# Fifty-six products behind the last one of a spectral mixing and MoE kernel

## The chip, the cores and the metric

The kernel runs on one core of a Trainium2 chip. The metric is the device time of one execution in microseconds (us), from the program's first instruction to its last; the time of a kernel is the median of several runs. Engines are named as the profile names them: PE is TensorE's products and PEld its weight loads, DVE is VectorE, ACT is ScalarE, POOL is GpSimd, SP is SyncE; SPq and ACTq are the queues from which transfers (DMAs) are issued.

## The reference

The input `x` is 8 x 3136 x 256. It goes through a real Fourier transform along 3136, a complex 256 x 256 mixing with bias, a soft threshold and the inverse transform. A second part mixes along the sequence at rank 32 and along the channels by a two-layer network, with a residual.

```python
X = np.fft.rfft(x, axis=1)
Yr = Xr @ w_r - Xi @ w_i + b_r
Yi = Xr @ w_i + Xi @ w_r + b_i
Yr = np.sign(Yr) * np.maximum(np.abs(Yr) - lam, 0.0)     # the same for Yi
y = np.fft.irfft(Y, n=x.shape[1], axis=1)
h = y.transpose(0, 2, 1) @ U @ V
u = y + h.transpose(0, 2, 1)
out = u + np.maximum(u @ w_ch1, 0.0) @ w_ch2
```

## The kernel before, in words

The transform of 3136 = 49 x 64 points is done as products with constant matrices in four steps (a, b, c, d in the names `psa`, `psb`, `psc`, `psd`, with the mixing in `psq` and `pst` between b and c). The channel network works on 49 windows of 512 tokens: its first layer writes `psx`, `psy` and `psz`, its second layer the two banks `pso` (`l2_chunks`, lines 1567 to 1595). Most products are in fp32r and in three parts, high by high, low by high and high by low, so that nearly fp32 accuracy comes out; some are in plain fp32, and the profile shows two instructions for each of those.

The Python code first records all operations in a `_Program` (line 165). Its `order` (line 255) plans them with costs and due times, and `trace` (line 506) then gives them out in the order of their planned starts; so nearly all instructions of the profile carry line 517. After `prog.order()` in line 1714 the pools are opened, and line 1721 gives the program out. The pool `ps_f` has three PSUM banks with the tags `psf.0` to `psf.2`; the pools `ps_m` and `ps_o` hold the other banks.

The end of the program is this. The second layer of the last window in turn, window 47, ends with a chunk whose six products are sorted so that the bank `pso_0` is complete before `pso_1` (line 1582). `o_unit` (line 1598) adds each bank to the window `xq` on VectorE, `out_unit` (line 1606) transposes each half into the tile `os`, and four transfers take `os` to the output, two from the queue of SyncE and two from the queue of ScalarE (line 1616). After that the program closes with a barrier over the five engines. The last use of the banks `psf.*` is the rank-32 product `psv` of that window, some 30 us ahead of the end. The first-layer weights lie in `w1t`, 128 partitions with 7 x 2 x 512 numbers each.

Of the kernel before, what the change touches and what calls it, by code (L numbers as in the profile page):

```python
# [13 lines left out]
F32 = mybir.dt.float32  # L14
# [150 lines left out]
class _Program:  # L165
# [339 lines left out]
    def trace(self, engines, junk):  # L505
        def real(v):
            return v.get() if isinstance(v, _View) else v

        for op in sorted(self.ops, key=lambda o: (o.start, o.n)):
            if op.fill:  # L510
                o = op.out.buf.get()
                while len(o.shape) > 2:
                    o = o[:, 0]
                for _ in range(op.fill):
                    engines["pe"].matmul(o[:, 0:128], lhsT=junk, rhs=junk, start=True, stop=True)
            call = getattr(engines[op.eng], op.name)
            call(*[real(a) for a in op.args], **{k: real(a) for k, a in op.kw.items()})  # L517


@with_exitstack  # L520
def fft_mix_moe_kernel(
# [19 lines left out]
    nc = tc.nc  # L541
    prog = _Program()
    act, dve, pool, pe, dma = [prog.engine(e) for e in ("act", "dve", "pool", "pe", "sp")]
    const, dram = _Pool("const", 1), _Pool("dram", 1, "dram")
    ps_f, ps_m, ps_o = _Pool("ps_f", 3, "psum"), _Pool("ps_m", 1, "psum"), _Pool("ps_o", 1, "psum")
# [42 lines left out]
    w1t = const.tile([128, 7, 2, 512], F32R, name="w1t", tag="w1")  # L588
# [1078 lines left out]
    for w, prev, next_w in zip(turn_w, [None] + turn_w, turn_w[1:] + [None]):  # L1667
        b, j = divmod(w, NW)
        if j == 0 and b < NB:
            assert not side  # L1670
            side = [(6.5, lambda b=b: rest_unit(b))]
            if b + 1 < NB:
                start, mid, end = (1, 58, 84) if b else (18, 71, 86)
# [13 lines left out]
        for g in range(2):  # L1687
            l1s = l1_chunks(w, g)
            new = l2_chunks(w, g)
            for k in range(4):  # L1690
                for c in range(2):
                    n = WS * j + 8 * g + 2 * k + c
# [26 lines left out]
    make_identity(nc, ident.get())  # L1719
    with tc.manual_schedule():  # L1720
        prog.trace(engines, ident.get())


def _dft_constants():
# [81 lines left out]
```

## Time and profile before

| | us |
|---|---|
| median of three runs | 1691.04 |
| lowest and highest of them | 1690.72, 1691.92 |
| the profiled execution, from first to last instruction (its span) | 1691.6 |
| PE busy in it | 1678.4 (99%) |
| DVE busy in it | 1320.9 (78%) |
| mean granted TensorE clock | 0.996 of full speed |

The page lists nothing of the profiled execution outside its span, so the span stands for its own time; it is 0.56 us above the median. In the views, a row of the timeline gives the start, the duration, the engine, the line, the operation, what is written and read (`pso<-rl,w2t` is written into `pso` from `rl` and `w2t`), the shapes and a count. Products overlap: each of 512 columns shows a duration of about 0.40 us, while its neighbour starts 0.23 us later. So the rate of a series is read from its starts, and the duration of one product tells when the last of a series is finished.

### The profile page before, as it was taken

What the parts mean: (1) busy time and instruction counts of PE and PEld (TensorE: products, weight loads), DVE (VectorE), ACT (ScalarE), POOL (GpSimd) and SP (SyncE); (2) the same over time, 40 slices, a digit from 0 to 9 for tenths busy, and PEclk for the clock granted to TensorE, in tenths of its full rate; (3) what the DMA queues carried; (4) which work ended last, traced back from release to release, by engine and by line L of the source; (5) the groups of instructions that cost most, each with busy time, mean ns of one, the idle gap of its engine ahead of it and who ended that gap; (6) DMA issues with size and microseconds to landing.
All of it is one profiled execution on the core that took longest, in us unless ns stands there. A gap on an engine that the chain in (4) does not pass through costs nothing.

```text
span 1691.6 us, 31458 instructions
## 1 busy us (share of the span) xinstructions
PE 1678.4 (99%) x11104; PEld 1513.1 (89%) x11104; DVE 1320.9 (78%) x2487; ACT 1015.6 (60%) x2187; POOL 574.7 (34%) x502
## 2 busy tenths in 40 slices
PE   9999999999999999999999999999999999999998
PEld 6979998999898998999988989999989999998887
DVE  7788898589856989679875788868985689866775
ACT  4765765556666665556666666555666566554443
POOL 2312553133534443123443444223343233312221
PEclk9989999999999999999999999999999999999999
DMA  9763444324553444413464344422455234420221
GB/s 260 240 220 90 136 128 125 96 73 116 157 170 111 127 141 117 121 51 89 118 193 132 118 141 121 137 59 74 120 155 167 76 92 110 114 69 10 77 57 38
DMA packets 243449, 200.64 MB, mean 119 GB/s; under 512 B 131387, under 2 KB 192609, under 8 KB 243293
## 3 DMA queue, kind: packets, MB, share of 16 engines
q1 hardware_dynamic: 240654, 197.77, 40.9%
q8 instruction: 89, 1.46, 0.4%
q10 hardware_dynamic: 2638, 0.86, 0.2%
q14 instruction: 68, 0.55, 0.1%
HBM read 121.36 MB, written 77.20 MB: 117 GB/s over the span
## 4 chain that ended last, share of the span: by engine, by line
PE 97%; DMA 1%; DVE 1%; issue 0%; SPq 0%; ACT 0%; DVEq 0%
PE pso L517 32%; PE psy L517 18%; PE psx L517 8%; PE psq L517 7%; PE psd L517 7%; PE psa L517 6%; PE psb L517 5%; PE psc L517 4%; PE psz L517 4%; PE pst L517 4%; PE psv L517 1%; DMA xx<-in_x_dram 0%; DMA fb<-in_fb_dram 0%; PE psu L517 0%; DMA out_dram<-os 0%; DVE t0t L517 0%
## 5 line engine op out<-in xcount | busy, mean ns | idle before, releaser
L517 PE MATMUL pso<-rh,w2t 128*128 128x512 f32 x1568 | 433.6, 398 | 0.0
L517 PEld LDWEIGHTS pso<-rh,w2t 128*128 128x128 f32 x1568 | 275.6, 188 | 44.5
L517 PE MATMUL pso<-rl,w2t 128*128 128x512 f32 x784 | 246.9, 396 | 0.3 <-DVE rl L517 0.3
L517 DVE SCALAR_TENSOR_TENSOR ys<-tb,rl 64x256 f32<-64x256 f32 x350 | 197.4, 564 | 12.2 <-ACT rl L517 6.8
L517 POOL TENSOR_TENSOR yl<-ys,yh 128x512 fp32r<-128x512 f32 (+1 forms) x101 | 137.3, 1359 | 189.6 <-ACT yh L517 172.1
L517 POOL TENSOR_TENSOR xl<-xt,xh 98x512 fp32r<-98x512 f32 x96 | 130.1, 1355 | 207.0 <-ACT xh L517 195.9
L517 PEld LDWEIGHTS pso<-rl,w2t 128*128 128x128 f32 x784 | 147.6, 188 | 35.7 <-DVE rl L517 0.7
L517 DVE SCALAR_TENSOR_TENSOR rl<-s,rh 128x512 fp32r<-128x512 f32 x196 | 155.8, 801 | 5.1 <-ACT rh L517 2.9
L517 ACT ACTIVATE rh<-s 128x512 fp32r<-128x512 f32 x196 | 121.7, 629 | 57.8 <-DVE s L517 56.6
L517 POOL TENSOR_TENSOR tl<-ts,th 128x256 fp32r<-128x256 f32 x88 | 71.2, 810 | 203.9 <-ACT th L517 140.3
L517 PE MATMUL psq<-wmt,xsh 128*128 128x256 f32 (+1 forms) x704 | 130.3, 282 | 0.0
L517 PE MATMUL psy<-odh,w1t 128*128 128x256 f32 x784 | 126.3, 283 | 0.0
L517 DVE TENSOR_TENSOR v<-v,psy 128x512 f32<-128x512 f32 x98 | 67.2, 685 | 73.7 <-ACT v L517 63.8
L517 PEld LDWEIGHTS psy<-odh,w1t 128*128 128x128 f32 x784 | 113.5, 189 | 9.9
L517 PEld LDWEIGHTS psq<-wmt,xsh 128*128 128x128 f32 (+1 forms) x704 | 112.0, 188 | 5.3 <-ACT gs L517 0.2
L517 PE MATMUL psd<-dt,zt 98*128 98x130 f32 x896 | 115.3, 275 | 0.5 <-DVE os L517 0.5
L517 PEld LDWEIGHTS psd<-dt,zt 98*128 98x128 f32 x896 | 111.0, 191 | 4.7 <-issue 0.7
L517 ACT ACTIVATE xsh<-psb 128x256 fp32r<-128x256 f32 (+1 forms) x176 | 60.5, 381 | 89.8 <-PE psb L517 87.5
L517 ACT ACTIVATE xq<-psd 128x196 f32<-128x196 f32 x256 | 82.1, 332 | 47.3 <-PE psd L517 35.7
L517 DVE TENSOR_TENSOR pa<-pa,psd 128x64 f32<-128x64 f32 x248 | 54.2, 219 | 67.9 <-ACT xq L517 58.9
L517 ACT ACTIVATE v<-psx 128x512 f32<-128x512 f32 x98 | 58.6, 598 | 76.8 <-PE psx L517 70.6
L517 POOL TENSOR_TENSOR ocl<-xq,och 128x256 fp32r<-128x256 f32 x47 | 37.8, 803 | 195.6 <-ACT och L517 182.6
(215 smaller groups left out, 4283.3 us busy)
## 6 DMA issues: line engine op xcount, KB each, us to landing
zt<-zd SPq DMA_DIRECT2D x128, 196.0 KB
zd<-zs SPq DMA_DIRECT2D x192, 128.0 KB
out_dram<-os SPq DMA_DIRECT2D x190, 128.0 KB
t<-gd SPq DMA_DIRECT2D x168, 128.0 KB
xt<-in_x_dram SPq DMA_DIRECT2D x100, 196.0 KB
gd<-gs SPq DMA_DIRECT2D x96, 196.0 KB
fb<-in_fb_dram SPq DMA_DIRECT2D x96, 128.0 KB
vw<-vd SPq DMA_DIRECT2D x96, 128.0 KB
```

The source lines that it names most:

```text
L517: call(*[real(a) for a in op.args], **{k: real(a) for k, a in op.kw.items()})
```

## The change

Behind the last operation of the program a new function gives out products whose results nothing reads. They read the first-layer weights in `w1t` and write three new tiles in the banks `psf.0` to `psf.2`. The words that came with the change speak of 60 products; the code has 56. In their order: five with 512 columns and 128 outputs; five with 72 outputs; five whose moving operand takes every second number (`two`); five that jump between two places 256 numbers apart (`cross`); five that take the same two numbers again and again (`same`); sixteen over 64 partitions, alternately the lower and the upper half, into two banks in turn, eight of 512 and eight of 256 columns; six of the same kind in plain fp32 with 64 columns; four in plain fp32 over 64 partitions into 64 output partitions, with 256 columns, one for each quarter of the array; and five of 512 columns that start one number further on.

```diff
+def more_idle(nc, pool, w):
+
+    o = [pool.tile([128, 512], F32, tag=f"psf.{k}", bufs=1, name=f"psidle_{k}") for k in range(3)]
+    lhsT = w[:, 4096:4224]
+
+    def mm(out, lhsT, rhs):
+        nc.tensor.matmul(out, lhsT=lhsT, rhs=rhs, start=True, stop=True, skip_group_check=True)
+
+    two = w[:, 0:1024].rearrange("p (n t) -> p t n", t=2)
+    cross = w[:, 0:512].rearrange("p (t n) -> p n t", t=2)
+    same = w[:, 0:2].unsqueeze(1).broadcast_to([128, 256, 2])
+    for _ in range(5):
+        mm(o[0], lhsT, w[:, 0:512])
+    for _ in range(5):
+        mm(o[0][:72], w[:, 4096:4168], w[:, 0:512])
+    for _ in range(5):
+        mm(o[0], lhsT, two[:, 0])
+    for _ in range(5):
+        mm(o[0].rearrange("p (n t) -> p n t", t=2), lhsT, cross)
+    for _ in range(5):
+        mm(o[0].rearrange("p (n t) -> p n t", t=2), lhsT, same)
+    for n in (512, 256):
+        for k in range(8):
+            r = 64 * (k % 2)
+            mm(o[1 + k % 2][:, :n], w[r : r + 64, 4096:4224], w[r : r + 64, 0:n])
+    f = w.bitcast(F32)
+    for k in range(6):
+        r = 64 * (k % 2)
+        mm(o[1 + k % 2][:, :64], f[r : r + 64, 4096:4224], f[r : r + 64, 0:64])
+    for k in range(4):
+        r, c = 64 * (k // 2), 64 * (k % 2)
+        mm(o[1 + k // 2][c : c + 64, :256], f[r : r + 64, 4096:4160], f[r : r + 64, 0:256])
+    for _ in range(5):
+        mm(o[0], lhsT, w[:, 1:513])
...
     with tc.manual_schedule():
         prog.trace(engines, ident.get())
+        more_idle(nc, ps_f.real, w1t.get().rearrange("p a b c -> p (a b c)"))
```

What stands on TensorE at the end of the program, as a piece of the difference (`psidle` are the new tiles, `w1t` the weights; a count is of products in a row):

```order
 L517 MATMUL pso_1_20951<-rh_1_1_21012,w2t 128x512 x2
 L517 MATMUL pso_1_20951<-rl_1_1_21019,w2t 128x512
-L1801 UNCONDITIONAL_BRANCH
+L526 MATMUL psidle_21069<-w1t 128x512 x5
+L526 MATMUL psidle_21069<-w1t 72x512 x5
+L526 MATMUL psidle_21069<-w1t 128x512 x15
+L526 MATMUL psidle_21070<-w1t 128x512
+L526 MATMUL psidle_21071<-w1t 128x512
```

Where the program branched to its end right behind the last product of `pso`, the new products now stand, without a wait on any of them, and the branch stands behind the last of them.

What stands on GpSimd at the same place, where the barrier of the five engines is gathered:

```order
 L517 TENSOR_TENSOR obl_20819<-xq_16_19055,obh_20800 128x512 [waits PE_49,Activation_49]
 L517 TENSOR_TENSOR odl_20862<-tt_20758,odh_20853 128x512 [waits PE_49,Activation_49]
-L1801 UNCONDITIONAL_BRANCH
-L1801 ISA [waits barrier_Pool_Activation_PE_DVE_SP_gather]
+L1838 UNCONDITIONAL_BRANCH
+L1838 ISA [waits barrier_Pool_Activation_PE_DVE_SP_gather]
```

Only the line numbers differ here. VectorE, ScalarE and SyncE also carry the same instructions with the same waits as before.

## The prediction

> **What bounds the kernel now.** I read the page first, for who carries the chain that ended last:
>
> ```profile
> span 1691.6 us, 31458 instructions
> PE 1678.4 (99%) x11104; PEld 1513.1 (89%) x11104; DVE 1320.9 (78%) x2487; ACT 1015.6 (60%) x2187; POOL 574.7 (34%) x502
> PE 97%; DMA 1%; DVE 1%; issue 0%; SPq 0%; ACT 0%; DVEq 0%
> ```
>
> TensorE bounds the kernel for 97% of the chain. But the change stands behind TensorE's last product, so only the end matters, and there the chain of waits, in order of time, leaves TensorE:
>
> ```profile
> 1677.58 6.33 PE pso L517 x27
> ...
> 1684.00 0.70 DVE xq L517
> ...
> 1684.72 0.71 DVE os L517
> 1685.43 0.59 DVE xq L517
> ...
> 1686.04 0.71 DVE os L517
> ```
>
> The timeline of the last microseconds shows when TensorE is done and what comes after:
>
> ```profile
> 1683.73 0.63 PE L517 MATMUL pso<-rh,w2t 128*128 128x512 f32 x2
> ...
> 1684.00 0.69 DVE L517 TENSOR_TENSOR xq<-xq,pso 128x512 f32<-128x512 f32 x1 [5.06 <-PE pso L517]
> 1684.19 0.40 PE L517 MATMUL pso<-rl,w2t 128*128 128x512 f32 x1
> ...
> 1685.36 0.65 DVE L517 TENSOR_TENSOR xq<-xq,pso 128x512 f32<-128x512 f32 x1
> ...
> 1686.78 0.85 SPq L517 DMA_DIRECT2D out_dram<-os  x2
> 1686.78 0.93 ACTq L517 DMA_DIRECT2D out_dram<-os  x2
> ```
>
> The last product starts at 1684.19 and ends at 1684.59. VectorE adds and transposes both halves until 1686.75, then four transfers of `os` are issued. The windows say when those land (columns: stretch, length, busy time of five engines, granted clock, DMA share, GB/s):
>
> ```profile
> 1687.00:1688.00 1.00, 0.00 (x0) 0.00 (x0) 0.00 (x0) 0.00 (x0) 0.00 (x0) 1.00 0.26 69
> 1688.00:1689.00 1.00, 0.00 (x0) 0.00 (x0) 0.00 (x0) 0.00 (x0) 0.00 (x0) 1.00 0.70 187
> 1689.00:1690.00 1.00, 0.00 (x0) 0.00 (x0) 0.00 (x0) 0.00 (x0) 0.00 (x0) 0.70 1.16 263
> 1690.00:1690.50 0.50, 0.00 (x0) 0.00 (x0) 0.00 (x0) 0.00 (x0) 0.00 (x0) 0.50 0.06 11
> 1690.50:1691.60 1.10, 0.00 (x0) 0.00 (x0) 0.00 (x0) 0.00 (x0) 0.00 (x0) 0.50 0.00 0
> ```
>
> After 1690.0 only 11 GB/s for 0.5 us, some 5 KB, is left, so the data have moved by about 1690.1; until 1691.6 the program closes. TensorE thus stands idle from 1684.59 to the end, 7.0 us. That is the cover for the new products.
>
> **The change, term by term.** The order shows 56 new products, not 60, with no wait among them, and the gather barrier that GpSimd waits for at the end takes TensorE in. So the end is the later of two paths: the output path, 1691.6 as now, and TensorE's list plus the closing. I need the length of the list.
>
> *Thirty products over 128 rows with 512 columns* (plain, 72 outputs, three other patterns, an offset start; five each). The chain has 27 such products in 6.33 us, 0.234 each, and the last three start 0.23 apart. 30 x 0.234 = 7.02. Fewer output columns save nothing by the nearest row, 64 of them:
>
> ```profile
> 1445.90 0.40 PE L517 MATMUL psq<-wmt,xsh 128*64 128x256 f32 x2
> 1446.13 0.28 PE L517 MATMUL psq<-wmt,xsl 128*64 128x256 f32 x1
> ```
>
> Two products of 256 columns take 0.23, as with 128 outputs:
>
> ```profile
> 1671.28 0.71 PE psx L517 x6
> ```
>
> That is 0.71 / 6 = 0.118 for 256 columns.
>
> *Sixteen half-array products* (64 rows, alternately the lower and the upper half, on two banks): one after another 8 x 0.234 + 8 x 0.118 = 1.87 + 0.94 = 2.81.
>
> *Ten in plain fp32*, each run as two instructions, six of 64 columns on halves and four of 256 on quarters. Small ones are priced by these rows:
>
> ```profile
> 1431.31 1.05 PE L517 MATMUL psb<-fb,t 128*128 128x128 f32 x8
> 1432.12 0.37 PE L517 MATMUL pst<-wm0h,th 128*128 128x256 f32 x1
> ...
> 80.55 1.49 PE L517 MATMUL psu<-us,fdt 98*98 98x32 f32 x16
> 81.88 1.08 PE L517 MATMUL psa<-xa,fas 98*98 98x512 f32 x2
> 82.39 0.68 PE L517 MATMUL psy<-b4r,one 128*128 128x256 f32 x1
> 82.91 0.28 PE L517 MATMUL psy<-wm0h,x3w 128*128 128x256 f32 x1
> ```
>
> Eight instructions of 128 columns take 1432.12 - 1431.31 = 0.81, 0.101 each; sixteen of 32 columns take 1.33, 0.083 each. For 64 columns I take 0.09: 12 x 0.09 = 1.08. A product of 512 fp32 columns and one of 256 behind it take 82.91 - 81.88 = 1.03; less 0.118 that is 0.91, so 0.455 for 256 columns: 4 x 0.455 = 1.82.
>
> *Changes between whole array and parts.* One place of the trace has products over 64 rows:
>
> ```profile
> 1440.75 0.28 PE L517 MATMUL psq<-wmt,xsl 128*128 128x256 f32 x1
> ...
> 1440.95 0.52 PEld L517 LDWEIGHTS psb<-fb,t 64*128 64x128 f32 x4
> 1440.95 0.71 PE L517 MATMUL psb<-fb,t 64*128 64x128 f32 x4
> ...
> 1441.59 0.19 PEld L517 LDWEIGHTS pst<-wm0h,th 128*128 128x128 f32 x1
> ```
>
> The weights wait for the product before (0.20 instead of 0.118 behind it), and the next whole-array weights wait until 0.64 after the four began, instead of 4 x 0.101 = 0.40. That makes 0.08 + 0.24 = 0.32 for in and out; with one more change, halves to quarters, 0.40.
>
> One after another the list is 7.02 + 2.81 + 1.08 + 1.82 + 0.40 = 13.13.
>
> *Do neighbouring halves run side by side?* No row shows it: the 64-row place uses one half only. The bounds are nothing saved and half (a quarter for the quarters), down to what the instructions need to start. Neighbours share no rows, no bank, no weights, and weight loads already run beside products (89% and 99% of the span busy), so I take side by side: 512 columns 8 x 0.117 = 0.94; 256 columns not under 0.083 each, 0.66; fp32 halves 12 x 0.083 = 1.00; quarters, eight instructions, 0.66. The list: 7.02 + 0.94 + 0.66 + 1.00 + 0.66 + 0.40 = 10.68. [...]
>
> *The other patterns.* The nearest rows for scattered reads:
>
> ```profile
> L517 PE MATMUL psa<-xx,fa 98*128 98x512 f32 x32 | 14.3, 596 | 1.1 <-DMA xx<-in_x_dram 1.1
> L517 PE MATMUL psa<-xt,fas 98*98 98x512 f32 x8 | 4.0, 601 | 0.0
> ...
> L517 DVE STREAM_TRANSPOSE os<-xq 128x512 f32<-128x512 f32 x96 | 65.5, 697 | 7.9 <-DMA out_dram<-os 7.1 <-DMA zt<-zd 0.3
> L517 DVE STREAM_TRANSPOSE t0t<-psa 128x512 f32<-128x512 f32 x16 | 14.7, 1030 | 9.9 <-PE psa L517 9.9
> ```
>
> TensorE reads `xx` in runs of 16 numbers at no loss (596 against 601 ns). VectorE, on single scattered numbers, is 1030 / 697 = 1.48 times slower. So 15 products in the three patterns cost between nothing and 0.48 x 15 x 0.234 = 1.7. I take one pattern of the three, the one that jumps 1 KB at each step (`cross`), at about 1.5: 5 x 0.117 = 0.6.
>
> *What stands beside it.* The output path is not moved; the same VectorE operations, transfers and queues stand in it. The products write other banks than VectorE reads; its first add, beside a running product, took 0.69 and the second, alone, 0.65, so four operations lose 0.16 at most, on a path that is no longer last.
>
> **The sum.** The first idle product starts 0.23 behind the last real one, 1684.42. Plus 10.68 + 0.6 the last slot ends at 1695.70, and its product drains 0.40 - 0.23 = 0.17 longer: 1695.87. That is 5.8 past the landing of the output, so TensorE is what the barrier waits for. The closing behind it lies between nothing and the 1.5 us that follow the landing now; that stretch also holds the completion of the transfers, so I take 0.6. The end: 1696.47, against 1691.6, +4.9. The median of the runs, 1691.04, is 0.56 under the profiled execution; on it +4.87 gives 1695.9.
>
> **The rivals.**
>
> *One after another.* The halves share the one array. List 13.13, 2.45 longer: 1698.4. For it: no overlapping pair anywhere in the trace. Against: nothing that two neighbours share. 22%.
>
> *The jumping pattern is much dearer.* At half speed the five products add 1.17, at a quarter 3.51, instead of 0.6: 1696.5 to 1698.8. [...] No row of this trace has TensorE reading so. 14%.
>
> *Hidden after all: not slower.* The cover is 7.0 us up to the end; about 0.2% (3.4 us) is what a measurement of this kernel can tell from no change. So the list, drain and closing must fit in 1695.0 - 1684.42 = 10.6. With 0.17 and a closing of 0.3 the list must be under 10.1. With no price for patterns, no changes of mode (-0.40), and halves and quarters that overlap fully (512 columns 0.94, 256 columns 0.47, fp32 halves 12 x 0.045 = 0.54, quarters 0.455) it is 9.42, the end 1694.3, on the median 1693.8. Against: the thirty whole products alone use 7.02, and the weight loads have a price. 11%; with the lower edges of the other cases I give 15% to no change.
>
> *VectorE is held.* If the release of its adds came only behind the whole list, the 7.0 us now behind the last product would follow 1695.87: 1702.9, on the median 1702.3. For it: VectorE's rows wait for TensorE by one semaphore. Against: the waits of VectorE's rows are the same in both orders. 2%.
>
> *Less is run than is written*, because nobody reads it: then 1691.0. The built order holds the 56 products, so 1%.
>
> **How the numbers follow.** The likeliest case, side by side with a small price for patterns, has 50%: 1695.9, its own range 1694.3 to 1697.4 (closing 0 to 1.5, patterns 0 to 1.2, changes of mode 0 to 0.4). The range of 8 in 10 runs from the hidden case, 1693.8, to one after another with `cross` at half speed and the whole closing, 1698.4 + 0.6 + 0.9 = 1699.9; I end it at 1699.7. Faster by over 0.2%: nothing is taken out, 2%. Within: 15%. Slower: 83%.
>
> **What would show it.** In the profile after: `psidle` products from 1684.4 on; the last ending between 1694 and 1699; 0.234 between starts of the plain ones; for the halves, two starts within 0.234 (right) or one (wrong); `cross` at 0.234 or more; VectorE's four operations and the last transfers where they were. It is wrong if the output path ends later than now, or if the span's end follows TensorE by more than 1.5 us.

## The result, and the profile after

The changed kernel took 1698.2 us (median of five runs, 1696.02 to 1700.56) against 1691.04; the ratio is 1.0040, with a 95% interval of 1.0026 to 1.0054, so it is slower by 4.4 to 9.1 us. Measured once more beside other kernels (eleven runs) the ratio was 1.0027 (1.0018 to 1.0036), 3.0 to 6.1 us. The forecast difference, +4.9 us, lies in both; the forecast level, 1695.9, is 2.3 us under the first median and 0.1 under the second, 1696.02.

The page of the profile after, from its head:

```profile
span 1693.9 us, 31590 instructions
PE 1685.3 (99%) x11170; PEld 1517.5 (90%) x11170; DVE 1323.8 (78%) x2487; ACT 1015.1 (60%) x2187; POOL 574.9 (34%) x502
```

TensorE has 66 instructions more, 46 products of one and 10 of two. The chain of waits, in order of time, no longer leaves TensorE at the end:

```profile
1679.80 2.33 PE pso L517 x10
1682.12 10.92 PE psidle L526 x61
```

The timeline of the end shows both paths (start, duration, engine, line, what is written and read, shapes, count):

```profile
1681.53 0.69 DVE L517 TENSOR_TENSOR xq<-xq,pso 128x512 f32<-128x512 f32 x1 [5.06 <-PE pso L517]
1681.73 0.39 PE L517 MATMUL pso<-rl,w2t 128*128 128x512 f32 x1
1681.96 11.08 PE L526 MATMUL psidle<-w1t 128*128 128x512 f32 x66
...
1682.89 0.65 DVE L517 TENSOR_TENSOR xq<-xq,pso 128x512 f32<-128x512 f32 x1
...
1684.32 0.85 SPq L517 DMA_DIRECT2D out_dram<-os  x2
1684.32 0.93 ACTq L517 DMA_DIRECT2D out_dram<-os  x2
```

The transfers are issued 1684.32 - 1681.73 = 2.59 us behind the start of the last real product, as before (1686.78 - 1684.19 = 2.59): VectorE's adds wait for nothing new, and cost the same 0.69 and 0.65. The idle products start without a wait on their banks, whose last product `psv` had started at 1651.2 in the profile before, some 40 us ahead of its end and not 30. They run on until 1693.04. In the windows (busy time of PE, PEld, DVE, ACT, POOL, then clock, DMA share and GB/s) the output has long landed by then:

```profile
1687.00:1688.00 1.00, 1.00 (x6) 0.89 (x5) 0.00 (x0) 0.00 (x0) 0.00 (x0) 1.00 0.64 142
1688.00:1689.00 1.00, 1.00 (x6) 0.61 (x7) 0.00 (x0) 0.00 (x0) 0.00 (x0) 1.00 0.00 0
...
1691.60:1693.90 2.30, 1.44 (x9) 0.87 (x5) 0.00 (x0) 0.00 (x0) 0.00 (x0) 1.00 0.00 0
```

From the end of the last product to the end of the span, 1693.93, the closing takes 0.89 us.

One number must be read with care. The last real product starts at 1681.73 here and at 1684.19 in the profile before, though nothing ahead of it differs. In ten profiles with the same program ahead of it, this start lies between 1680.8 and 1686.1, with a mean granted clock of 0.996 to 0.999 in the four late ones (1683.7 and after) and of 1.000 in the six early ones (up to 1682.6); a cause was not tested. That scatter is as large as the effect. So the kernels are compared below by the time **from the start of the last real product to the end of the span**: 7.36 us before (1684.19 to 1691.56, before rounding), 1693.93 - 1681.73 = 12.20 after, 12.20 again in the second profile. The change costs 4.84 us there.

### The profile page after: what moved, and what is told of

Its sections match the earlier page's. It is cut to its first block, busy times and chain, and to the rows that moved or that the text cites. A ratio compares the mean times of both kernels' runs of the same rounds, so it can differ in the third digit from the quotient of the medians.

```text
span 1693.9 us, 31590 instructions
## 1 busy us (share of the span) xinstructions
PE 1685.3 (99%) x11170; PEld 1517.5 (90%) x11170; DVE 1323.8 (78%) x2487; ACT 1015.1 (60%) x2187; POOL 574.9 (34%) x502
## 4 chain that ended last, share of the span: by engine, by line
PE 97%; DMA 2%; DVE 1%; ACT 0%; POOL 0%; issue 0%; SPq 0%; DVEq 0%
PE pso L517 32%; PE psy L517 18%; PE psx L517 8%; PE psq L517 7%; PE psd L517 7%; PE psb L517 5%; PE psa L517 5%; PE psz L517 4%; PE psc L517 4%; PE pst L517 4%; PE psv L517 1%; PE psidle L526 1%; DMA xx<-in_x_dram 0%; DMA fb<-in_fb_dram 0%; DMA zt<-zd 0%; DMA fas<-in_fa_dram 0%
```

## The experiments

The theory of the list: the end is the later of two paths, the output path (7.36 us) and TensorE's list of idle products with 0.23 ahead and the drain and the closing behind; halves in other rows run side by side (in the changed kernel two of 512 columns start every 0.23 us). Its rivals: a standing cost of any products at the end (suggested by the 7.2 us between the medians), VectorE held behind the list, and part-array products that are short wherever they stand. The first four experiments were timed together with 21 runs of the kernel before, whose median was 1693.33 us; since single runs scatter by several us (those 21 from 1690.12 to 1695.83), the quotient of two medians differs from the ratios given by up to about 0.001. The others have one run with its profile each.

**Twenty plain products.**

```diff
-    two = w[:, 0:1024].rearrange("p (n t) -> p t n", t=2)
...
-    for _ in range(5):
-        mm(o[0], lhsT, w[:, 1:513])
+    for _ in range(20):
+        mm(o[0], lhsT, w[:, 0:512])
```

> The 56 products are replaced by 20 plain ones over the whole array. Theory of the list: 20 x 0.234 = 4.7 us, done some 0.8 us before the last transfer lands, so no change: ratio 1.000, within 0.1%. Rival, a standing cost that any products at the end bring (the median moved by 7.2 us where the two profiles explain 4.8): about 2.4 us, ratio 1.0014. Rival, VectorE is held behind the list: 4.7 us, ratio 1.0028.

Measured: 1692.34 us, ratio 1.000 (0.9991 to 1.0009). The timeline of its end:

```profile
1686.08 0.39 PE L517 MATMUL pso<-rl,w2t 128*128 128x512 f32 x1
...
1686.31 4.73 PE L526 MATMUL psidle<-w1t 128*128 128x512 f32 x20
...
1688.67 0.85 SPq L517 DMA_DIRECT2D out_dram<-os  x2
```

The products end at 1691.04, 4.96 us behind the last real start; the span ends at 1693.43, 7.35 behind it. They are hidden. The held VectorE is out (transfers again 2.59 behind); a standing cost of 2.4 us lies outside the interval.

**The changed kernel again.**

> The changed kernel once more. Theory of the list: 10.9 us of products and 0.9 us of closing in place of the output path, 4.8 us more than before, ratio 1.0029. Rival, a standing cost on top: 7.2 us again, ratio 1.0042.

Measured: 1696.02 us, ratio 1.0027 (1.0018 to 1.0036). That excludes 1.0042 (the quotient of the two medians is still lower, 1.0016); with the 12.20 us in the profile again, the 7.2 us between the first medians hold some 2 us of scatter.

**The list twice.**

```diff
+    for _twice in range(2):
         for _ in range(5):
             mm(o[0], lhsT, w[:, 0:512])
...
```

> The whole list twice, 112 products. Theory of the list: each product past the cover counts in full, so 10.9 us more than the changed kernel, 15.7 us over before, ratio 1.0093. Rival, a standing cost on top: 18.1 us, ratio 1.0107. If the list were hidden in part by something else than the output path, less than 15 us.

Measured: 1706.65 us, ratio 1.0092 (1.0078 to 1.0106); 23.10 us from the last real product to the end, 10.9 more than the changed kernel. Its chain of waits:

```profile
1679.00 3.03 PE pso L517 x13
1682.03 21.83 PE psidle L526 x123
```

21.83 is twice 10.92: past the cover every product counts in full.

**All parts in one place.**

```diff
-            r = 64 * (k % 2)
+            r = 0
...
-        r, c = 64 * (k // 2), 64 * (k % 2)
+        r, c = 0, 0
```

> The same 56 products, but all halves on the lower-numbered half of the rows and all quarters on one quarter, banks still alternating. Theory that neighbours run side by side only because they use other rows and columns: 512 columns 8 x 0.234 instead of 0.92 us, 256 columns 8 x 0.118 instead of 0.47, fp32 halves 12 x 0.10 instead of 0.67, quarters 4 x 0.455 instead of 0.49: 3.2 us more than the changed kernel, 8.0 over before, ratio 1.0047. Rival, that half-size products are simply shorter wherever they stand: no more than the changed kernel, 4.8 us, ratio 1.0029.

Measured: 1700.7 us, ratio 1.0051 (1.0038 to 1.0064); 15.54 us from the last real product to the end, 3.34 more than the changed kernel. The chain of waits:

```profile
1678.89 2.33 PE pso L517 x10
1681.22 14.26 PE psidle L526 x66
```

The list is 14.26 instead of 10.92. The timeline in a short stretch among the halves shows why, here in one place

```profile
1689.15 0.62 PE L526 MATMUL psidle<-w1t 64*128 64x512 f32 x2
...
1692.43 0.59 PE L526 MATMUL psidle<-w1t 64*64 64x256 f32 x2
```

and in the changed kernel:

```profile
1689.36 0.63 PE L526 MATMUL psidle<-w1t 64*128 64x512 f32 x4
...
1691.01 0.45 PE L526 MATMUL psidle<-w1t 64*64 64x256 f32 x4
```

A row merges the products under way in its stretch: two halves lie within 0.62 us in one place, four within 0.63 in two places, two of them at a time; and four instructions on four quarters, within 0.45, start together. In one place a half of 512 columns still takes 0.23 us from start to start, as a whole product does: a part by itself was not shorter.

**Twenty-six plain products**, where both paths should meet (20 replaced by 26 in the first experiment).

> 26 plain products in place of the 56. The end of the span now lies 7.36 us behind the start of the last real product where the output path decides, and 0.23 + list + 0.17 + 0.89 where TensorE decides. 26 x 0.234 = 6.08 makes 7.37: the two paths meet. Theory of the list: 7.36 to 7.45 from the last real product to the end, against 7.35 with 20 products and 12.2 with the changed kernel. Rival, the two paths get in each other's way at the barrier: 7.6 or more.

Measured by one profile: 7.36 us. From its timeline:

```profile
1683.74 0.39 PE L517 MATMUL pso<-rl,w2t 128*128 128x512 f32 x1
...
1683.97 6.09 PE L526 MATMUL psidle<-w1t 128*128 128x512 f32 x26
```

The list ends 1690.06 - 1683.74 = 6.32 behind the last real start; with 0.89 of closing that is 7.21, just under the output path. So 26 products are free here as 20 are, and with the two paths 0.15 us apart the end stays at 7.36.

**Halves in other orders.**

```diff
+    for k in range(8):
+        mm(o[1 + k % 2], *half[k % 2][1:])
+    for k in range(8):
+        mm(o[1 + k // 2 % 2], *half[k // 2 % 2][1:])
+    for k in range(8):
+        mm(o[k % 2], *half[0][1:])
+    for k in range(8):
+        if k % 2:
+            mm(o[1], *half[0][1:])
+        else:
+            mm(o[0], W, X)
+    for k in range(4):
+        c = 64 * (k % 2)
+        mm(o[1 + k % 2][c : c + 64, 0:256], f[:, 4096:4160], f[:, 0:256])
+    for k in range(4):
+        mm(o[1 + k % 2][0:64, 0:256], f[:, 4096:4160], f[:, 0:256])
```

> Other products in place of the 56, in groups: eight halves alternating lower and upper rows (512 columns); eight halves in the order two lower, two upper; eight halves all on the same rows; four whole products alternating with four halves; four plain fp32 products of 256 columns over 128 rows, alternately into the two halves of the output columns; four of these all into the same half. Theory of places (a product starts, in order, as soon as its rows and columns are free): 4 slots of 0.234, 0.94 us; two by two 5 slots, 1.17; the same rows 8 slots, 1.87; whole and half in turn 8 slots and a price for each change, 0.2 each, 3.4; the columns 2 x 0.45 and 4 x 0.45 us. Rival, that halves overtake one another: two by two also 0.94. Rival, that a change of mode costs nothing by itself: whole and half in turn 1.87.

Measured by one profile, from the timeline of short stretches in the second, third, fourth (two rows) and last two groups:

```profile
1683.91 0.63 PE L526 MATMUL psidle<-w1t 64*128 64x512 f32 x4
...
1685.07 0.61 PE L526 MATMUL psidle<-w1t 64*128 64x512 f32 x2
...
1687.17 0.50 PE L526 MATMUL psidle<-w1t 64*128 64x512 f32 x1
...
1687.60 0.50 PE L526 MATMUL psidle<-w1t 128*128 128x512 f32 x1
...
1690.66 0.60 PE L526 MATMUL psidle<-w1t 128*64 128x256 f32 x4
...
1691.52 0.59 PE L526 MATMUL psidle<-w1t 128*64 128x256 f32 x2
```

The order two by two took 0.93 us (1683.91 to 1684.84), four slots and not five: its rows start in pairs like those of the alternating order. Here the rival's figure, 0.94, fits, and the theory's 1.17 does not. The trace does not name the rows, so which products start together is not shown, and the reading takes it that they stand in the program as they are written, as those of the changed kernel do in the order shown ahead of the prediction. On the same rows, eight took 1.82. Whole and half in turn start 1687.60 - 1687.17 = 0.43 apart, 0.20 over the plain 0.23 at each change: the price of a change is real. With halves of the columns it is alike: four fp32 products took 0.91 us on both halves and 1.73 on one.

**Moving patterns.**

```diff
+    def step(s):
+        return w[:, 0 : 512 * s].rearrange("p (n t) -> p t n", t=s)[:, 0]
+    def far(t):
+        return w[:, 0:512].rearrange("p (t n) -> p n t", t=t)
+    four = w[:, 0:1024].rearrange("p (n t) -> p n t", t=4)
+    pair = four[:, :, 0:2]
+    even = four.rearrange("p n (u t) -> p n u t", t=2)[:, :, :, 0]
+    for rhs in (w[:, 0:512], step(2), step(3), step(4), step(8), even, pair, far(2), far(4), far(8), w[:, 0:512]):
...
+        for _ in range(6):
+            mm(out, lhsT, rhs)
```

> Other products in place of the 56: six each of 512 columns, whole array, with the moving operand plain; every 2nd, 3rd, 4th, 8th number in one step; every 2nd number as a pattern of two levels (the same numbers as the first, in the same order); two neighbours out of every four; turn by turn from 2, 4 and 8 places far apart; and plain again. Read is the time between starts. [...] Theory of the single step (any step other than 1 in a one-level pattern halves the speed): steps 2, 3, 4 and 8 all 0.45, the two-level form and the pairs 0.23.

Measured by one profile. One product of each from step 2 to far 8 (of step 8 the next one too), in the program's order, from the timeline of short stretches:

```profile
1684.87 0.63 PE L526 MATMUL psidle<-w1t 128*128 128x512 f32 x1
...
1687.57 0.63 PE L526 MATMUL psidle<-w1t 128*128 128x512 f32 x1
...
1690.31 0.65 PE L526 MATMUL psidle<-w1t 128*128 128x512 f32 x1
...
1692.99 0.61 PE L526 MATMUL psidle<-w1t 128*128 128x512 f32 x1
...
1693.42 0.61 PE L526 MATMUL psidle<-w1t 128*128 128x512 f32 x1
...
1695.63 0.63 PE L526 MATMUL psidle<-w1t 128*128 128x512 f32 x1
...
1698.34 0.63 PE L526 MATMUL psidle<-w1t 128*128 128x512 f32 x1
...
1700.36 0.38 PE L526 MATMUL psidle<-w1t 128*128 128x512 f32 x1
...
1701.83 0.44 PE L526 MATMUL psidle<-w1t 128*128 128x512 f32 x1
...
1704.16 0.67 PE L526 MATMUL psidle<-w1t 128*128 128x512 f32 x1
```

A single duration is longer than the spacing by the drain, 0.17 to 0.18 us: 0.40 for a plain product that is 0.23 from the next and 0.61 for step 8, whose two products start 1693.42 - 1692.99 = 0.43 apart. The spacings, read from the starts of all six, were: step 2, 3, 4 and 8 0.45, 0.45, 0.46 and 0.43; every second in two levels 0.45; pairs 0.45; far 2, 4 and 8 0.22, 0.27 and 0.49. The theory of the single step is met on steps 2, 3, 4 and 8, which cost about the same, and falls on the two-level form and the pairs, at 0.45 instead of 0.23.

**Runs.** What fits all but far 4 and 8 is an estimate of the author's from these spacings: 0.45 us, half speed, for numbers out of a group of four neighbours (16 bytes, counted from the start of `w1t`) that the product does not read whole. The expectation calls such a group a line; that it is four numbers long no run had shown up to here.

```diff
+    def runs(n, every, at=0):
+        v = w[:, at : at + 512 // n * every].rearrange("p (k t) -> p k t", t=every)
+        return v[:, :, 0:n]
+    twice = w[:, 0:256].unsqueeze(2).broadcast_to([128, 256, 2])
+    for rhs in (runs(4, 8), runs(4, 8, 2), runs(8, 16), runs(8, 16, 2), runs(16, 32), twice):
```

> Other products in place of the 56, six each of 512 columns over the whole array: runs of 4 numbers out of every 8, starting on a 16-byte line; the same starting 2 numbers into a line; runs of 8 out of 16 on a line and 2 into it; runs of 16 out of 32; each number twice. Theory of whole lines (half speed whenever a line is left before all four of its numbers are used, however far the next one is): runs of 4, 8 and 16 on a line 0.23 us, runs of 4 two into a line 0.45, runs of 8 two into a line between (half of their numbers lie in lines left early, 0.34), each twice 0.22. Rival, that every jump forward costs and a run makes up for it by its length: runs of 4 near 0.34 wherever they start, of 8 near 0.28, of 16 near 0.26. Rival, that only the share of skipped numbers counts: all runs 0.45.

Measured by one profile. One product of each, in that order:

```profile
1685.31 0.40 PE L526 MATMUL psidle<-w1t 128*128 128x512 f32 x1
...
1687.58 0.63 PE L526 MATMUL psidle<-w1t 128*128 128x512 f32 x1
...
1689.65 0.40 PE L526 MATMUL psidle<-w1t 128*128 128x512 f32 x1
...
1691.37 0.50 PE L526 MATMUL psidle<-w1t 128*128 128x512 f32 x1
...
1693.31 0.40 PE L526 MATMUL psidle<-w1t 128*128 128x512 f32 x1
...
1694.44 0.38 PE L526 MATMUL psidle<-w1t 128*128 128x512 f32 x1
```

The spacings, 0.23, 0.45, 0.23, 0.33, 0.24 and 0.22, are those that the theory expected; runs of four took 0.23 us where they start at a multiple of eight numbers and 0.45 two numbers further on. The runs show these times and not how the operand is read. Both rivals fall. For three numbers out of every four, where the same theory expects 0.34 us for 384 columns (0.45 x 384 / 512), there is no measurement. Why alternating among four or eight places takes 0.27 and 0.49 and between two 0.22 was not shown.

## Why the prediction was right

**The mechanism was right.** The output path and TensorE's list race to the barrier, and 20, 26, 56 and 112 products give 7.35, 7.36, 12.20 and 23.10 us: flat up to the cover, then every microsecond of the list counts. The plain whole products and the side-by-side halves came out as argued (no run had shown halves side by side; the forecast took them so as an estimate, and in the changed kernel pairs of 512 columns start 0.23 us apart); the changes between whole array and parts cost 0.51 instead of 0.40. One premise for the parts does not hold for the quarters: two by two they share rows and a bank, and all four started together all the same.

**The sum was right partly because errors cancelled.** From the starts of the products in the changed kernel's timeline, without the 0.23 ahead, which was met:

| term | predicted us | measured us |
|---|---|---|
| thirty whole products with the pattern price | 7.02 + 0.60 | 7.91 |
| fp32r halves, 512 and 256 columns | 0.94 + 0.66 | 1.40 |
| fp32 halves | 1.00 | 0.62 |
| fp32 quarters | 0.66 | 0.48 |
| changes between whole array, halves and quarters | 0.40 | 0.51 |
| the list | 11.28 | 10.92 |
| drain of the last product | 0.17 | 0.16 |
| closing | 0.60 | 0.89 |
| from the last real start to the end, with 0.23 | 12.28 | 12.20 |

*The step that failed* is the choice among patterns: "one pattern of the three, the one that jumps 1 KB at each step (`cross`), at about 1.5". The timeline of the changed kernel, two products of `two` and two of `cross`:

```profile
1684.70 0.63 PE L526 MATMUL psidle<-w1t 128*128 128x512 f32 x1
...
1685.15 0.63 PE L526 MATMUL psidle<-w1t 128*128 128x512 f32 x1
...
1686.96 0.38 PE L526 MATMUL psidle<-w1t 128*128 128x512 f32 x1
...
1687.17 0.38 PE L526 MATMUL psidle<-w1t 128*128 128x512 f32 x1
```

`two` starts every 0.45 us, nearly twice the plain 0.23, and `cross` every 0.22: the price stood on the wrong pattern. Five times 0.22 for `two`, less a little for `cross` and `same`, made 0.89 over 7.02, where 0.60 was put. That this term still came within 0.3 us is luck. The factor of 1.48 behind the 0.60 was no price of TensorE's: its row, `t0t<-psa` (1030 ns), is VectorE reading a PSUM bank, and the row beside it, `os<-xq` (697), reads SBUF, so scattered numbers are not all that differs between them.

*The parts were too dear.* The floor of 0.083 an instruction, from fp32 products one after another, was laid on every instruction, though halves run side by side: 256 columns ran at 0.117 for two, fp32 of 64 columns at 0.11 for two. In one place each of these takes as long alone, 0.118 and 0.112. That took 0.76 off three terms.

*The closing was too short by 0.29*, inside its bounds.

**The rivals.** One after another would have been 1.0051, as the fourth experiment shows by forcing it, and is 3.34 us away in the profile. Hidden is what 26 products are, and 56 are not. VectorE was not held, and all 66 instructions ran. The half speed of the rival on the jumping pattern, 1.17 us for five products, is near what was found, 1.1, but on `two` and not on `cross` (0.45 and 0.22 us from start to start).

**The level.** The forecast let the span of the profiled execution stand for its time, 0.56 us over the median. In the runs after, a run's time lies some 2 us above its span (1696.02 beside 1693.93), so the span of 1691.6 before belongs to a time near 1693.7, some 2.6 over that median and not 0.56. That moved no term of the difference.

## What to carry to other kernels

Work added behind the last result was free here as long as its engine's list and the closing stayed under the output path (7.35 and 7.36 us with 20 and 26 products, 12.20 with 56); measure both from the last common instruction, since the scatter ahead of it, 1680.8 to 1686.1 here, can exceed the effect. Products on half the rows or half the columns paid only where their neighbours used the other half (0.93 against 1.82 us for eight, 0.91 against 1.73 for four in fp32), and each switch between whole and half products cost about 0.2 us. The halves that ran side by side wrote to different banks; halves of the rows into one bank were not tested, while two quarters that shared one did start together. For a moving operand in fp32r, the only type tested so, take runs of 4 or 8 numbers that start at a multiple of eight: they cost 0.23 us, two numbers further on 0.45 and 0.33, and a step of 2 as much (0.45) as a step of 8 (0.43).

## What the runs showed of the hardware

- A contiguous 512-column fp32r product starts every 0.231 us, while one that reads each number twice, the same two numbers, or alternates between two places starts every 0.216 to 0.218. What makes the difference was not tested.
- Eight halves of 512 columns, written two by two on different rows, took 0.93 us, four times the 0.23 from pair to pair in the alternating order; on the same rows eight took 1.82.
- Of an fp32r moving operand of 512 columns, steps of 2, 3, 4 and 8 and pairs out of four took 0.43 to 0.46 us from start to start; runs of 4 and 8 took 0.23 where they start at a multiple of eight numbers, and 0.45 and 0.33 where they start two numbers further on.
